# Row one-hots laid out by tile, a scan for the second half's places, and three first layers issued in a row

## The chip, the cores and the metric

The kernel runs on one core of one Trainium2 chip. The metric is device time in microseconds, the median of several executions. In the profile PE is TensorE (matmuls), PEld its weight loads, DVE is VectorE, ACT is ScalarE, POOL is GpSimd and SP is SyncE; a queue name such as POOLq is the engine's instruction sequencer.

## The reference

Attention without a softmax, and then a mixture of experts with one expert per token:

```
phi(x)  = outer product of S1 x and S2 x            # 8 x 8 = 64 features per head
kv, z   = sum over s of phi(k) v ,  sum of phi(k)   # 4 batches, 4 heads, 1088 positions, head_dim 32
x       = phi(q) kv / (phi(q) z + 1e-6)             # 4352 tokens x 128
expert  = argmax of cosine(x, expert_emb) / tau     # 8 experts
gate    = softmax of these logits at that expert
out     = gate * relu(x w1[expert]) w2[expert]      # 128 -> 1024 -> 128, float32
```

## The kernel before

**Two halves.** The four batches are worked as two halves (m = 0 and 1), each of 17 token tiles of 128 tokens. For each half the attention gives x and logits per token (steps `nd`, `x`), and a router finds each token's expert and its place in a list that is sorted by expert.

**The router** (`router`, line 728) works for half 0 on all 17 tiles at once and for half 1 on 8 and then on 9 tiles (`SPANS`). `best` and `pick` make a one-hot `oh` of the expert per token and its count `total`. `place` lets PE sum one-hots: `before` (a triangle of ones) times `oh` counts the tokens ahead in the same tile, and `ones` times shifted slices of `oh` adds the tiles ahead, one matmul per tile. `take` and `split` pick each token's own column out of the sum and split it into a block number `place_k` and a row `place_r`. `mark` compares `place_r` with the lane numbers and so writes `row`, a one-hot over 128 rows for every tile. In `row[P, P, tiles]` the tile number is the innermost index, 36 of them, so the 128 numbers of one tile lie 36 elements apart.

**The table** (`table`, lines 840 to 875). `sums` multiplies `row` of a tile (as weights, bfloat16, 128 x 128) with a few columns that carry the token numbers; summed over tiles that lists the tokens of each block. It is run once over 17 tiles for the first 10 blocks and once over 34 tiles for the other 25.

**The blocks.** 35 blocks of 128 tokens follow. Per block: `fetch` (POOL gathers the rows by an indirect DMA), `turn` (PE transposes them, DVE or ACT copies them out), `up` (first layer on PE, ReLU on ACT), `norm`, `shares`, `share` (the gate, on ACT, POOL and DVE) and `down` (second layer on PE, scaling on ACT, and an indirect DMA by POOL that scatters the result). Blocks 30, 31 and 32 are shared by two experts each (`two`, line 1069): `up` then uses column tiles of 64 with two weight sets, `down` column tiles of 32 (blocks 30 and 31) or 64 (block 32). Their second weights for `down` are copied by ACT (`second_weights_b`), into two buffers in turn.

**Order.** Nothing is scheduled by a planner: each step is put at a tick and a rank (`put_at`), ticks are emitted in order and ranks inside a tick, and every engine runs its instructions in the order in which they were emitted. Block i has tick 10 + i. In a tick the ranks are: `up` 30, `turn` of the next block 45, `shares` 60, `share` 73, `down` of the block before 74, `norm` of a later block 74.6, loads of weights 79. `fetch(34)` has rank 29 of block 30's tick. So on PE the order of the last blocks is up 30, turn 31, down 29, up 31, turn 32, down 30, up 32, turn 33, down 31, up 33, turn 34, down 32, up 34, down 33, down 34. Line 1256 puts a `drain` on POOL in block 32's tick, ahead of all other steps of that tick; on POOL the order is there: scatter 29, norm 33, scatter 30, norm 34, drain, scatter 31, 32, 33 and 34.

**The early part.** `ORDER` lists the steps of tick 4 by name. On DVE, ahead of half 1's feature product `qp 1`, come half 0's `take`, `split`, `rest`, the two `mark` and `find`; PE needs `qp 1` for the transposes `trqp 1`. `constants` (line 293) is the first step of all and `lanes` (line 330) stands after half 0's `total`.

Of the kernel before, what the change touches and what calls it, by code (L numbers as in the profile page):

```python
# [19 lines left out]
P = 128  # L20
# [51 lines left out]
def kernel(  # L72
# [195 lines left out]
    lane = consts.tile([P, P], F32, name="lane")  # L268
    lanes = consts.tile([P, P, WIDE], BF16, name="lanes")
    digits = consts.tile([P, 2, NM * NCP], BF16, name="digits")  # L270
# [10 lines left out]
    ones_e = consts.tile([P, E], F32, name="ones_e")  # L281
    oh = {(m, c): consts.tile([P, c1 - c, E], BF16, name=f"oh{m}_{c}") for m in range(NM) for c, c1 in SPANS[m]}
    total = {(m, c): consts.tile([P, E], BF16, name=f"total{m}_{c}") for m in range(NM) for c, _ in SPANS[m]}
# [46 lines left out]
    def wide_lanes():  # L330
        nc.vector.tensor_scalar_mul(lanes, bview(lane, [[1, P], [0, WIDE]]), 1.0 / P)

# [395 lines left out]
    def router(m, c0, c1, g, bank):  # L728
# [8 lines left out]
        def pick():  # L737

            t = work.tile([P, n, E], F32, tag=f"lt_{n}", name="lt")
# [4 lines left out]
            last["oh"] = nc.vector.tensor_tensor(out=oh[m, c0], in0=t, in1=mx.unsqueeze(2).broadcast_to([P, n, E]),  # L744
                                                 op=ALU.is_equal)
            with nc.allow_low_precision(reason="a count of at most SPAN is whole in bfloat16"):
                nc.vector.reduce_sum(out=total[m, c0], in_=oh[m, c0].rearrange("p j e -> p e j"), axis=AX.X)

        def place():

            hot = oh[m, c0]
            ps = s["ps"] = bank()[:, :n * E].rearrange("p (j e) -> p j e", e=E)
            mm(ps, before, hot, start=True, stop=False)
            for t in [base, less] + counts:
                mm(ps, ones, t.unsqueeze(1).broadcast_to([P, n, E]), start=False, stop=False)
            for j in range(1, n):
                mm(ps[:, j:], ones, hot[:, j - 1:j].broadcast_to([P, n - j, E]), start=False, stop=j == n - 1)
            counts.append(total[m, c0])  # L760

        def take():
            s["t"] = work.tile([P, n, E], F32, tag=f"lt_{n}", name="lt")
            nc.vector.tensor_mul(s["t"], s["ps"], oh[m, c0])

        def split():

            t0, t1 = m * NCP + c0, m * NCP + c1
            f = work.tile([P, n], F32, tag=f"mx8_{n}", name="mx8")
            nc.vector.reduce_sum(out=f, in_=s["t"], axis=AX.X)  # L770
            nc.vector.tensor_scalar(place_k[:, t0:t1], f, WHOLE, -WHOLE, op0=ALU.add, op1=ALU.add)
            nc.vector.scalar_tensor_tensor(out=place_r[:, t0:t1], in0=f, scalar=(P - 1) / (2.0 * P), in1=place_k[:, t0:t1],
                                           op0=ALU.add, op1=ALU.subtract)
# [54 lines left out]
    def table(which, m1, key):  # L828
# [21 lines left out]
        def sums():  # L850
            s["ps"] = ps_small()[:, :2 * n]
            tiles = [m * NCP + c for m in range(m1) for c in range(NC)]
            mm(s["ps"], ones, nowhere[which].rearrange("p d n -> p (d n)"), start=True, stop=False)
            for t in tiles:
                mm(s["ps"], row[:, :, t], s["col"].rearrange("p d n w -> p w d n")[:, t].rearrange("p d n -> p (d n)"),
                                 start=False, stop=t == tiles[-1])
# [46 lines left out]
    def plan_late():  # L903
# [94 lines left out]
        def extra():  # L998
# [29 lines left out]
            for t in tiles:  # L1028
                mm(ps, row[:, :, t], hit[:, 1:, t], start=False, stop=t == tiles[-1])
            with nc.allow_low_precision(reason="whole numbers of at most NOWHERE"):  # L1030
# [16 lines left out]
    def turn(i):  # L1047
        ps = ps_small()
        tp(ps[:, :P], xs[i][:, :DM], ident)
        xT[i] = work.tile([P, P], F32, tag="xTb", name="xTb")  # L1050
        (nc.scalar.copy if i < 2 or 4 <= i <= 8 else nc.vector.tensor_copy)(xT[i], ps[:, :P])  # L1051
# [17 lines left out]
    def two(i):  # L1069
        return FULL <= i < FULL + SHARED  # L1070
# [11 lines left out]
    def second_b(i):  # L1082
        return v_flat[1][:, i % 2 * F:(i % 2 + 1) * F]

# [7 lines left out]
    def up(i):  # L1092
        ps = ps_big()
        hT[i] = work.tile([P, 2, 512], F32, tag="kp", bufs=3, name="hT")
        x, w = xT.pop(i), wb.pop(i)
# [209 lines left out]
```

## Time and profile before

| | |
|---|---|
| runs | 196.45, 196.55, 197.93 us; median 196.55 us |
| profiled execution | 199.14 us, its span 197.2 us |
| PE busy | 188.3 us (95%), 2667 matmuls |
| PE weight loads | 177.8 us (90%) |
| POOL, ACT, DVE busy | 107.6, 99.1, 87.9 us |
| granted TensorE clock | 1.0 in every stretch read |

The span is what the trace shows of one execution; the profiled execution's own time is 1.94 us more, which lies around the span. Durations in the rows below are those of this one execution, whose time is above the median of the three others.

### The profile page before, as it was taken

How to read it: one execution, taken by the hardware profiler on the slowest of the kernel's cores; microseconds unless marked ns; L12 is line 12 of the kernel's file. 1: busy time of each engine (PE TensorE's matmuls, PEld its weight loads, DVE VectorE, ACT ScalarE, POOL GpSimd, SP SyncE). 2: the span in 40 equal slices, each digit the busy share in tenths (PEclk: the TensorE clock that was granted, in tenths of full speed). 3: DMA queues.
4: the chain of work that ended last, by engine and by line, in shares of the span. 5: the costliest groups of instructions: out<-in, count | busy, mean ns of one | idle time of the engine just before them, and what ended most of it. 6: DMA issues, size and time to landing. Idle time of an engine off the chain costs nothing.

```text
span 197.2 us, 7104 instructions
## 1 busy us (share of the span) xinstructions
PE 188.3 (95%) x2667; PEld 177.8 (90%) x2667; DVE 87.9 (45%) x393; ACT 99.1 (50%) x280; POOL 107.6 (55%) x135
## 2 busy tenths in 40 slices
PE   7999899999979999999999999999999999999990
PEld 7677799788869999999999999999999999998890
DVE  6589868798378489922221221221221221222100
ACT  2675542437253456433564654654654654766430
POOL 4300054707713866565977767767767767733052
PEclk9999999999999999999999999999999999999999
DMA  5979968974799997544587686596665655540001
GB/s 139 345 203 276 237 172 221 331 232 124 201 281 330 285 338 209 188 136 149 149 263 237 158 288 201 155 281 211 161 195 182 160 200 180 150 137 12 3 20 32
DMA packets 29924, 38.32 MB, mean 194 GB/s; under 512 B 5721, under 2 KB 23394, under 8 KB 29890
## 3 DMA queue, kind: packets, MB, share of 16 engines
q1 hardware_dynamic: 27600, 33.18, 56.3%
q0 software_dynamic: 2240, 4.67, 7.6%
q8 instruction: 23, 0.38, 0.8%
q14 instruction: 11, 0.09, 0.2%
q10 hardware_dynamic: 50, 0.01, 0.0%
HBM read 33.25 MB, written 4.66 MB: 192 GB/s over the span
## 4 chain that ended last, share of the span: by engine, by line
PE 75%; DMA 12%; DVE 6%; issue 2%; ACT 2%; POOLq 1%; POOL 0%
PE ps_big L155 35%; PE ps_acc L155 14%; PE ps_ab L155 14%; DMA xs<-rows,dst_i 12%; PE ps_t L158 6%; PE ps_t L155 3%; PE ps_acc L111 1%; DVE xg L679 1%; DVE row L779 1%; PE ps_ab L158 1%; PE ps_acc L158 1%; POOLq L1300 1%; DVE qp L458 1%; PE ps_big L158 1%; ACT hT L1108 1%
## 5 line engine op out<-in xcount | busy, mean ns | idle before, releaser
L155 PE MATMUL ps_big<-xTb,wb 128*128 128x128 f32 (+2 forms) x608 | 70.6, 266 | 0.1
L155 PEld LDWEIGHTS ps_big<-xTb,wb 128*128 128x128 f32 (+1 forms) x608 | 66.7, 183 | 1.5 <-issue 0.9
L1149 POOL DMA_INDIRECT out_dram<-y,dst_i x35 | 36.4, 1041 | 42.3 <-ACT sq L1113 21.4
L1108 ACT ACTIVATE hT<-ps_big 128x1024 f32<-128x1024 f32 x35 | 35.8, 1023 | 41.3 <-issue 23.6
L1043 POOL DMA_INDIRECT xs<-rows,dst_i x35 | 36.7, 1048 | 13.0 <-issue 6.1
L155 PE MATMUL ps_acc<-w_sb,hT 128*128 (+2 forms) x288 | 35.1, 275 | 0.0
L1051 DVE COPY xTb<-ps_t 128x128 f32<-128x128 f32 x28 | 8.1, 291 | 57.3 <-issue 39.7
L155 PEld LDWEIGHTS ps_acc<-w_sb,hT 128*128 128x128 f32 (+2 forms) x288 | 33.3, 184 | 0.3 <-issue 0.2
L155 PE MATMUL ps_ab<-w_sb,hT 128*128 (+1 forms) x272 | 33.2, 275 | 0.0
L155 PEld LDWEIGHTS ps_ab<-w_sb,hT 128*128 128x128 f32 (+1 forms) x272 | 31.6, 187 | 0.1
L1114 POOL TENSOR_TENSOR norm<-norm,half_c 128x1 f32<-128x1 f32 x35 | 20.7, 595 | 5.2 <-ACT sq L1113 4.9
L1127 DVE TENSOR_SCALAR gate<-gate 128x1 f32<-128x1 f32 x35 | 5.3, 150 | 21.2 <-ACT probs L1124 19.7
L458 POOL TENSOR_TENSOR kp<-both 128x1024 f32<-128x1024 f32 (+1 forms) x4 | 7.2, 1812 | 12.5 <-ACT both L499 11.1
L155 PE MATMUL ps_big<-kz,held 128*64 128x82 f32 x256 | 10.7, 236 | 1.1 <-ACT xTb L1051 1.1
L1146 ACT ACTIVATE y<-ps_ab,gate 128x128 f32<-128x128 f32 x17 | 6.2, 367 | 10.9 <-PE ps_ab L155 7.1
L155 PEld LDWEIGHTS ps_big<-kz,held 128*64 128x64 f32 x256 | 9.5, 136 | 2.3 <-ACT hT L1108 1.3
L1113 ACT ACTIVATE sq<-xs 128x128 f32<-128x128 f32 x35 | 10.6, 302 | 1.5 <-DMA xs<-rows,dst_i 1.3
L1124 ACT ACTIVATE probs<-xs,norm 128x8 f32<-128x8 f32 x35 | 10.3, 295 | 1.3 <-DVE norm L1118 1.3
L1146 ACT ACTIVATE y<-ps_acc,gate 128x128 f32<-128x128 f32 x17 | 6.2, 366 | 9.4 <-PE ps_acc L155 7.0
L158 PE MATMUL ps_t<-ident,xs 128*128 128x128 f32 x35 | 9.8, 279 | 0.0
L425 ACT COPY qT<-ps_t 128x512 f32<-128x512 f32 (+1 forms) x10 | 5.1, 535 | 7.2 <-PE ps_t L158 7.2
L458 DVE TENSOR_TENSOR kp<-both 128x1024 f32<-128x1024 f32 (+1 forms) x6 | 6.4, 1088 | 2.9 <-ACT both L499 2.8
(254 smaller groups left out, 254.4 us busy)
## 6 DMA issues: line engine op xcount, KB each, us to landing
wb<-in_moe_w_dram SPq DMA_DIRECT2D x35, 512.0 KB
w_sb<-in_moe_w_dram SPq DMA_DIRECT2D x16, 256.0 KB
rows<-xg SPq DMA_DIRECT2D x4, 544.0 KB
q<-in_q_dram SPq DMA_DIRECT2D x6, 256.0 KB
k<-in_k_dram SPq DMA_DIRECT2D x3, 512.0 KB
held<-in_moe_w_dram SPq DMA_DIRECT2D x3, 512.0 KB
v<-in_v_dram SPq DMA_DIRECT2D x2, 512.0 KB
v<-in_v_dram SPq DMA_DIRECT2D x4, 256.0 KB
```

The source lines that it names most:

```text
L155: last["pe"] = nc.tensor.matmul(*args, **how)
L158: last["pe"] = nc.tensor.transpose(*args)
L458: last[tag] = engine.tensor_mul(t.rearrange("p j h (i k) -> p (j h) i k", i=R), ab[:, :, 0].unsqueeze(3).broadcast_to([P, n * H, R, R]), b ...
L1043: nc.gpsimd.indirect_dma_start(out=xs[i][:], out_offset=None, in_=rows[:2 * S if t == 0 else N + 1], in_offset=bass.IndirectOffsetOnAxis(a ...
L1051: (nc.scalar.copy if i < 2 or 4 <= i <= 8 else nc.vector.tensor_copy)(xT[i], ps[:, :P])
L1108: nc.scalar.activation(hT[i], ps, ACT.Relu)
L1113: nc.scalar.activation(sq, xs[i][:, :DM], ACT.Square, accum_out=norms[i])
L1114: nc.gpsimd.tensor_tensor(out=norms[i], in0=norms[i], in1=half_c, op=ALU.pow)
L1124: nc.scalar.activation(p, xs[i][:, DM:], ACT.Exp, scale=norms.pop(i)[:, 0:1], accum_out=gate[i])
L1127: nc.vector.tensor_scalar_add(gate[i], gate[i], PROB_EPS)
L1146: nc.scalar.activation(y, ps, ACT.Copy, scale=gate.pop(i)[:, 0:1])
L1149: d = nc.gpsimd.indirect_dma_start(out=out[:, :], out_offset=bass.IndirectOffsetOnAxis(ap=dst_i[t][:, j:j + 1], axis=0), in_=y[:], in_offs ...
```

## The change

- `row` becomes `[P, tiles, P]`: the 128 numbers of a tile lie side by side. `place_r` holds each value twice and `lanes` shrinks from 128 x 10 to 128, so that `mark` can compare in pairs.
- For half 1, `oh` is laid out by expert and then tile. A scan along the tiles (`tensor_tensor_scan`, which restarts at each expert by a factor of 0 in `again`) gives running counts, `runs`; its last column is `total`. `place` then needs PE for the sum over tokens ahead in other lanes and over earlier spans alone, 8 columns wide: 4 matmuls for the first span and 5 for the second, in place of 11 and 13. DVE multiplies `runs` with `oh`, and `split` sums twice as many elements.
- The first layers of the shared blocks stand in a row. PE's order becomes up 29, turn 30, turn 31, down 28, turn 32, up 30, up 31, up 32, turn 33, turn 34, down 29, down 30, down 31, down 32, up 33, up 34, down 33, down 34. Block 32's transposed rows, its hidden layer and its second weights get places of their own; ACT's copies of second weights and one load of first weights come a tick earlier; the register loads for the shared blocks' second layers come before the down ahead of them.

```diff
-    lanes = consts.tile([P, P, WIDE], BF16, name="lanes")
+    lanes = consts.tile([P, P], BF16, name="lanes")
-    oh = {(m, c): consts.tile([P, c1 - c, E], BF16, ...)
+    oh = {(m, c): consts.tile([P, E, c1 - c] if m else [P, c1 - c, E], BF16, ...)
+    runs = {c: consts.tile([P, E, c1 - c], BF16, name=f"runs{c}") for c, c1 in SPANS[1]}
+    total = {(1, c): t[:, :, t.shape[2] - 1] for c, t in runs.items()}
-    place_r = consts.tile([P, NM * NCP], BF16, name="place_r")
-    row = consts.tile([P, P, NM * NCP], BF16, name="row")
+    place_r = consts.tile([P, NM * NCP, 2], BF16, name="place_r")
+    row = consts.tile([P, NM * NCP, P], BF16, name="row")
...
+        nc.vector.memset(upto_own, -(P + 1) / (2.0 * P))
+        for t in again.values():
+            nc.vector.memset(t, 1.0)
+            nc.vector.memset(t[:, :, :1], 0.0)
-        for t in (place_k, place_r):
-            nc.vector.memset(t, -1.0)
+        nc.vector.memset(place_k, -1.0)
...
 def pick():
+                if m == 0:
                     nc.vector.reduce_sum(out=total[m, c0], in_=oh[m, c0].rearrange("p j e -> p e j"), axis=AX.X)
+                else:
+                    nc.vector.tensor_tensor_scan(out=flat(runs[c0]), data0=flat(again[c0]), data1=flat(oh[m, c0]),
+                                                 initial=0.0, op0=ALU.mult, op1=ALU.add)
+        def place_by_runs():
+            ps = s["ps"] = bank()[:, :E]
+            mm(ps, before, total[m, c0], start=True, stop=False)
+            sums = [base, upto_own] + counts
+            for i, t in enumerate(sums):
+                mm(ps, ones, t, start=False, stop=i == len(sums) - 1)
+            counts.append(total[m, c0])
+            s["t"] = work.tile([P, 2, E, n], F32, tag=f"lt_{n}", bufs=1, name="pt")
+            nc.vector.scalar_tensor_tensor(out=s["t"][:, 0], in0=runs[c0], scalar=1.0 / P, in1=oh[m, c0],
+                                           op0=ALU.mult, op1=ALU.mult)
 def take():
+            if m == 1:
+                nc.vector.tensor_mul(s["t"][:, 1], oh[m, c0], s["ps"].unsqueeze(2).broadcast_to([P, E, n]))
+                s["t"] = s["t"].rearrange("p t e j -> p j (t e)")
+                return
 def mark(a=c0, b=c1):
-            w = b - a + (b - a) % 2
-            t0, t1 = m * NCP + a, m * NCP + a + w
-            nc.vector.tensor_tensor(out=row[:, :, t0:t1], in0=lanes[:, :, :w],
-                                    in1=bview(place_r[:, t0:t1], [[0, P], [1, w]]), op=ALU.is_equal)
+            w, t0 = b - a, m * NCP + a
+            nc.vector.tensor_tensor(out=row[:, t0:t0 + w].rearrange("p t (l d) -> p t l d", d=2),
+                                    in0=bview(lanes, [[0, w], [2, HALF], [1, 2]]),
+                                    in1=bview(place_r[:, t0:t0 + w], [[2, w], [0, HALF], [1, 2]]), op=ALU.is_equal)
 def sums():
-                mm(s["ps"], row[:, :, t], ...)
+                mm(s["ps"], row[:, t], ...)
 def turn(i):
+        if i == FULL + SHARED - 1:
+            xT[i] = v_rest[0][0][:, :H].rearrange("p h d -> p (h d)")
 def second_b(i):
-        return v_flat[1][:, i % 2 * F:(i % 2 + 1) * F]
+        m, u = ((1, 0), (1, 1), (0, 0))[i - FULL]
+        return v_flat[m][:, u * F:(u + 1) * F]
 def up(i):
+        if i == FULL + SHARED - 1:
+            hT[i] = v_flat[0][:, F:2 * F].rearrange("p (u n) -> p u n", u=2)
 def in_ticks(b0, b1, tick):
-                put(0, 29.9, lambda i=i: second_layers(i))
-                put(0, 30, lambda i=i: up(i))
-            if i + 1 < b1:
-                put(0, 45, lambda i=i: turn(i + 1))
+                to = put_at(tick + min(i, FULL) - b0) if two(i) else put
+                if two(i):
+                    put_at(tick + i - 1 - b0)(0, 73.8, lambda i=i: second_layers(i))
+                else:
+                    to(0, 29.9, lambda i=i: second_layers(i))
+                to(0, 30, lambda i=i: up(i))
+            j = i + 1
+            if 0 < j < b1:
+                to, rank = put, 45
+                if j == FULL + 1:
+                    to = put_at(tick + FULL - 1 - b0)
+                elif j == FULL + SHARED - 1:
+                    to, rank = put_at(tick + FULL - 1 - b0), 74.5
+                elif j >= FULL + SHARED:
+                    to, rank = put_at(tick + FULL - b0), 73.9
+                to(0, rank, lambda j=j: turn(j))
-                put(0, 74, lambda i=i: down(i - 1))
+                to = put_at(tick + min(i, FULL + SHARED - 1) - b0) if two(i - 1) else put
+                to(0, 74, lambda i=i: down(i - 1))
-                put(0, 79, lambda i=i: weights(i + 2))
+                to = put_at(tick + FULL - 1 - b0) if i + 2 == FULL + SHARED - 1 else put
+                to(0, 79, lambda i=i: weights(i + 2))
-                    put(1, 79, lambda i=i: second_weights_b(i + 2))
+                    put(0, 79, lambda i=i: second_weights_b(i + 2))
```

## Rows read from the trace of the kernel before

**Rows 1.** PE's waits: line, releaser, us in total, times, longest us.
```profile
PE ps_big L155 <- ACT xTb L1051: 1.1, 1, 1.1
```
**Rows 2.** Timeline of PE, half 1's second place: start us, us, instruction, count.
```profile
68.46 0.20 PE L155 MATMUL ps_big<-oh,before 128*128 128x72 bf16 x1
...
68.83 0.17 PE L155 MATMUL ps_big<-near,ones 128*128 128x8 bf16 x1
```
**Rows 3.** Timeline of PE, the second table's sums and the first layer behind them.
```profile
85.72 2.22 PE L155 MATMUL ps_t<-hits,row 128*128 128x56 bf16 x34
87.78 2.03 PE L155 MATMUL ps_big<-xTb,wb 128*128 128x128 f32 x16
```
**Rows 4.** Tile view of row: durations in ns, least, median, most; starts; forms.
```profile
L155 PEld LDWEIGHTS <-row x51: 137/169/180, 43.6 to 87.7; 128*128 128x128 bf16 x51
...
L779 DVE TENSOR_TENSOR row<-lanes,place_r x4: 684/762/818, 41.3 to 81.6; 128x1024 bf16<-128x1024 bf16 x2, 128x1280 bf16<-128x1280 bf16 x2
```
**Rows 5.** Timeline of PE's weight loads in half 1's first place.
```profile
64.45 0.34 PEld L155 LDWEIGHTS <-ones 128*128 128x128 bf16 x10
```
**Rows 6.** Timeline of DVE: start us, us, instruction [idle before, released by].
```profile
2.39 0.17 DVE L227 TENSOR_SCALAR s_w<-swords 16x32 uint32<-16x32 uint32 x1 [0.25 <-DMA swords<-in_S_dram]
...
26.31 1.23 DVE L458 TENSOR_TENSOR kp<-both 128x1024 f32<-128x1024 f32 x1 [1.47 <-ACT both L499]
...
41.28 1.42 DVE L779 TENSOR_TENSOR row<-lanes,place_r 128x1024 bf16<-128x1024 bf16 x2
...
82.82 1.19 DVE L848 TENSOR_TENSOR hits<-hits,digits 128x1008 bf16<-128x1008 bf16 x1
```
**Rows 7.** Timeline of PE where it waits for DVE's qp.
```profile
45.09 1.09 PE L158 MATMUL ps_big<-ident,qp 128*128 128x128 f32 x8 [0.27 <-DVE qp L458]
```
**Rows 8.** Timeline of PE over the last blocks.
```profile
169.28 0.24 PE L155 MATMUL ps_big<-xTb,wb 128*64 128x32 f32 x1
...
169.50 0.19 PE L155 MATMUL ps_big<-xTb,wb 128*64 128x32 f32 x1
...
171.19 0.19 PE L155 MATMUL ps_big<-xTb,wb 128*64 128x32 f32 x1
...
171.79 0.33 PE L158 MATMUL ps_t<-ident,xs 128*128 128x128 f32 x1
...
176.31 0.33 PE L158 MATMUL ps_t<-ident,xs 128*128 128x128 f32 x1
176.56 0.30 PE L155 MATMUL ps_acc<-w_sb,hT 128*32 x1
...
178.45 0.27 PE L155 MATMUL ps_big<-xTb,wb 128*64 128x64 f32 x1
...
180.70 0.33 PE L158 MATMUL ps_t<-ident,xs 128*128 128x128 f32 x1
...
188.72 1.95 PE L155 MATMUL ps_ab<-w_sb,hT 128*128 x16
190.51 1.95 PE L155 MATMUL ps_acc<-w_sb,hT 128*128 x16
```
**Rows 9.** POOL's drain by its line: durations in ns, least, median, most; start.
```profile
L1256 POOLq DRAIN  x1: 7095/7095/7095, 179.3 to 179.3; - x1
```
**Rows 10.** Timeline of POOL, the scatters of blocks 30 to 32 and 34.
```profile
179.25 1.04 POOL L1149 DMA_INDIRECT out_dram<-y,dst_i  x1 [3.04 <-ACT sq L1113]
...
187.26 1.01 POOL L1149 DMA_INDIRECT out_dram<-y,dst_i  x1 [6.36 <-issue]
188.58 0.98 POOL L1149 DMA_INDIRECT out_dram<-y,dst_i  x1 [0.30 <-issue]
...
193.15 0.97 POOL L1149 DMA_INDIRECT out_dram<-y,dst_i  x1 [0.82 <-DVE y L1144]
```
**Rows 11.** Timeline of ACT, scaling of block 29 and a copy of second weights.
```profile
173.94 0.37 ACT L1146 ACTIVATE y<-ps_ab,gate 128x128 f32<-128x128 f32 x1 [0.70 <-PE ps_ab L155]
...
174.50 1.03 ACT L1087 COPY v<-w_sb 128x1024 f32 x1
```

More of the change, by code (lines that the diff above doesn't have):

```diff
@@ L281 @@
     ones_e = consts.tile([P, E], F32, name="ones_e")
-    oh = {(m, c): consts.tile([P, c1 - c, E], BF16, name=f"oh{m}_{c}") for m in range(NM) for c, c1 in SPANS[m]}
-    total = {(m, c): consts.tile([P, E], BF16, name=f"total{m}_{c}") for m in range(NM) for c, _ in SPANS[m]}
+    oh = {(m, c): consts.tile([P, E, c1 - c] if m else [P, c1 - c, E], BF16, name=f"oh{m}_{c}")
+          for m in range(NM) for c, c1 in SPANS[m]}
+    runs = {c: consts.tile([P, E, c1 - c], BF16, name=f"runs{c}") for c, c1 in SPANS[1]}
+    total = {(1, c): t[:, :, t.shape[2] - 1] for c, t in runs.items()}
+    total[0, 0] = consts.tile([P, E], BF16, name="total0")
+    again = {c: consts.tile([P, E, c1 - c], BF16, name=f"again{c}") for c, c1 in SPANS[1]}
+    upto_own = consts.tile([P, E], BF16, name="upto_own")
     c_early = consts.tile([P, E + 1], F32, name="c_early")
@@ L330, in wide_lanes @@
     def wide_lanes():
-        nc.vector.tensor_scalar_mul(lanes, bview(lane, [[1, P], [0, WIDE]]), 1.0 / P)
+        nc.vector.tensor_scalar_mul(lanes, lane, 1.0 / P)
     def digits_of():
@@ L737, in pick @@
         def pick():
-            t = work.tile([P, n, E], F32, tag=f"lt_{n}", name="lt")
+            t = work.tile([P, 1 + m, n, E], F32, tag=f"lt_{n}", name="lt", **({"bufs": 1} if m else {}))[:, 0]
             mx = work.tile([P, n], F32, tag=f"mx8_{n}", name="mx8")
@@ L743, in pick, with flat @@
             nc.vector.reduce_max(out=mx, in_=t, axis=AX.X)
[L744 to L747, printed above, removed]
+            last["oh"] = nc.vector.tensor_tensor(out=oh[m, c0].rearrange("p e j -> p j e") if m else oh[m, c0], in0=t,
+                                                 in1=mx.unsqueeze(2).broadcast_to([P, n, E]), op=ALU.is_equal)
+            with nc.allow_low_precision(reason="a count of at most NC is whole in bfloat16"):
+                if m == 0:
+                    nc.vector.reduce_sum(out=total[m, c0], in_=oh[m, c0].rearrange("p j e -> p e j"), axis=AX.X)
+                else:
+                    nc.vector.tensor_tensor_scan(out=flat(runs[c0]), data0=flat(again[c0]), data1=flat(oh[m, c0]),
+                                                 initial=0.0, op0=ALU.mult, op1=ALU.add)
+        def flat(t):
+            return t.rearrange("p e j -> p (e j)")
+        def place_by_runs():
[8 more added lines that the diff above has]
+                                           op0=ALU.mult, op1=ALU.mult)
         def place():
+            if m == 1:
+                return place_by_runs()
             hot = oh[m, c0]
@@ L762, in take @@
         def take():
-            s["t"] = work.tile([P, n, E], F32, tag=f"lt_{n}", name="lt")
+            if m == 1:
+                nc.vector.tensor_mul(s["t"][:, 1], oh[m, c0], s["ps"].unsqueeze(2).broadcast_to([P, E, n]))
+                s["t"] = s["t"].rearrange("p t e j -> p j (t e)")
+                return
+            s["t"] = work.tile([P, 1, n, E], F32, tag=f"lt_{n}", name="lt")[:, 0]
             nc.vector.tensor_mul(s["t"], s["ps"], oh[m, c0])
@@ L771, in split @@
             nc.vector.tensor_scalar(place_k[:, t0:t1], f, WHOLE, -WHOLE, op0=ALU.add, op1=ALU.add)
-            nc.vector.scalar_tensor_tensor(out=place_r[:, t0:t1], in0=f, scalar=(P - 1) / (2.0 * P), in1=place_k[:, t0:t1],
+            nc.vector.scalar_tensor_tensor(out=place_r[:, t0:t1], in0=f.unsqueeze(2).broadcast_to([P, n, 2]),
+                                           scalar=(P - 1) / (2.0 * P),
+                                           in1=place_k[:, t0:t1].unsqueeze(2).broadcast_to([P, n, 2]),
                                            op0=ALU.add, op1=ALU.subtract)
         def mark(a=c0, b=c1):
-            w = b - a + (b - a) % 2
-            t0, t1 = m * NCP + a, m * NCP + a + w
-            nc.vector.tensor_tensor(out=row[:, :, t0:t1], in0=lanes[:, :, :w],
-                                    in1=bview(place_r[:, t0:t1], [[0, P], [1, w]]), op=ALU.is_equal)
+            w, t0 = b - a, m * NCP + a
+            nc.vector.tensor_tensor(out=row[:, t0:t0 + w].rearrange("p t (l d) -> p t l d", d=2),
+                                    in0=bview(lanes, [[0, w], [2, HALF], [1, 2]]),
+                                    in1=bview(place_r[:, t0:t0 + w], [[2, w], [0, HALF], [1, 2]]), op=ALU.is_equal)
         def write():
@@ L854, in sums @@
             for t in tiles:
-                mm(s["ps"], row[:, :, t], s["col"].rearrange("p d n w -> p w d n")[:, t].rearrange("p d n -> p (d n)"),
+                mm(s["ps"], row[:, t], s["col"].rearrange("p d n w -> p w d n")[:, t].rearrange("p d n -> p (d n)"),
                                  start=False, stop=t == tiles[-1])
@@ L1028, in extra @@
             for t in tiles:
-                mm(ps, row[:, :, t], hit[:, 1:, t], start=False, stop=t == tiles[-1])
+                mm(ps, row[:, t], hit[:, 1:, t], start=False, stop=t == tiles[-1])
             with nc.allow_low_precision(reason="whole numbers of at most NOWHERE"):
@@ L1049, in turn @@
         tp(ps[:, :P], xs[i][:, :DM], ident)
-        xT[i] = work.tile([P, P], F32, tag="xTb", name="xTb")
+        if i == FULL + SHARED - 1:
+            xT[i] = v_rest[0][0][:, :H].rearrange("p h d -> p (h d)")
+        else:
+            xT[i] = work.tile([P, P], F32, tag="xTb", name="xTb")
         (nc.scalar.copy if i < 2 or 4 <= i <= 8 else nc.vector.tensor_copy)(xT[i], ps[:, :P])
@@ L1093, in up @@
         ps = ps_big()
-        hT[i] = work.tile([P, 2, 512], F32, tag="kp", bufs=3, name="hT")
+        if i == FULL + SHARED - 1:
+            hT[i] = v_flat[0][:, F:2 * F].rearrange("p (u n) -> p u n", u=2)
+        else:
+            hT[i] = work.tile([P, 2, 512], F32, tag="kp", bufs=3, name="hT")
         x, w = xT.pop(i), wb.pop(i)
@@ L1221, in in_ticks @@
             if i < b1:
-                put(0, 29.9, lambda i=i: second_layers(i))
-                put(0, 30, lambda i=i: up(i))
-            if i + 1 < b1:
-                put(0, 45, lambda i=i: turn(i + 1))
+                to = put_at(tick + min(i, FULL) - b0) if two(i) else put
+                if two(i):
+                    put_at(tick + i - 1 - b0)(0, 73.8, lambda i=i: second_layers(i))
+                else:
+                    to(0, 29.9, lambda i=i: second_layers(i))
[10 more added lines that the diff above has]
+                to(0, rank, lambda j=j: turn(j))
             if i < b1:
```

## The prediction

> **What bounds the kernel now.** I read the busy shares first: PE is busy 95% of the span, the others about half. Then PE's waits: its longest one behind the warm-up of the first microseconds is 1.1 us [rows 1], and the timeline shows no other of size. So from about 45 us on, PE's own work is the path, and what is taken from PE there comes off the end, as long as nothing else takes over. Two places break that rule. Between 38 and 45 us DVE is the path: it runs without a gap through half 0's take, split, marks and table, and PE waits 0.27 us for `qp 1` behind them [rows 7]. And at the very end the path is PE, then the scaling, then POOL's scatter of block 34 at 193.15 [rows 10], 0.85 us behind PE's last matmul (190.51 plus 1.79, the distance of the last two second layers [rows 8], is 192.30). From that scatter to the end of the span lie 4.05 us that no edit touches. The drain on POOL, 7.1 us long [rows 9], is off the path now: scatter 31 begins 8.01 us after scatter 30, two scatters in a row are 1.32 us apart [rows 10], so the queue alone would allow scatter 34 at 179.25 + 8.01 + 3 x 1.32 = 191.2. It has 1.9 us to spare.
>
> **The change part by part.**
>
> *The sums over 34 tiles.* 34 matmuls with `row` as weights take 87.78 - 85.72 = 2.06 us, 61 ns each [rows 3]. Their columns can't explain that: the 13 matmuls of half 1's second place, up to 72 columns wide, stand 0.37/13 = 28.5 ns apart [rows 2]. What differs is the weight load: 169 ns for `row` [rows 4], while ten loads of `ones`, whose numbers lie side by side, take 0.34 us together, as the union of overlapping loads [rows 5]. If the new layout brings `row` to the pace of `ones`, 34 x (61 - 28.5) = 1.09 us go, on PE's path. The bounds are 0 (the loads stay as they are) and 1.09; I take 1.09, since the other layout is the one visible difference. The first 17 sums shorten too, but PE only waits longer for `qp 1` there: nothing.
>
> The Trainium skill, "TensorE: Matmul & The Clock Gate", section "Weight-path perf modes", speaks against this: it lets the fast weight load apply to every non-FP32 load of 128 columns whose column step is between -1,023 and 1,024 elements, packed or strided. By that rule the old loads, at a step of 36, are fast already and nothing is won. The 169 ns row does not look like it, so I keep that as a rival.
>
> *Places.* 7 + 8 = 15 matmuls fewer at 28.5 ns: 0.43 us off PE's path. On DVE a scan replaces a sum over at most 72 elements, one product per span is added, and `split` sums twice as much: some 0.2 us each, for two spans. DVE waits for PE in this stretch, and after it the last product for the table ends at 84.01 [rows 6], 1.7 us before PE needs it at 85.72 [rows 3]; with PE 0.43 earlier 1.3 us of cover remain. Nothing; without that cover about 0.6 us.
>
> *Marks.* The trace has no compare in pairs. The old rows give (818 - 684)/256 = 0.52 ns per element above a fixed part [rows 4]. The new marks have 1024 and 1152 elements (the padding column goes). At the old pace half 0's pair loses 0.06 us, which I don't count; at twice that time per element it grows from 1.52 to 2.60, 1.08 us longer, all on DVE's path ahead of `qp 1`. I take no change, as both forms hold 16-bit neighbours.
>
> *Constants and lanes.* Five more small memsets and one less stand at the start, where DVE waits 0.25 us for the sketches' DMA; the smaller `lanes` frees DVE before 26.31, where it waits 1.47 us for ACT anyway [rows 6]. Both nothing; without the first cover a few tenths.
>
> *The moved transposes.* Turns 31 and 32 now precede up 30. One matmul of that size takes 1.79/16 = 0.11 us [rows 8]: 0.22 us later. Up 30 now starts at T = 169.28 [rows 8]; afterwards at T' = 169.28 - 1.09 - 0.43 + 0.22, 1.30 us earlier.
>
> *The row of three.* Six starts of a repeated group in up 30 span 171.19 - 169.50 = 1.69 us, 0.282 us each, so its eight would take 2.25; it took 2.51 up to the transpose [rows 8]. The 0.26 us at its end I read as the array running empty before it changes its tile shape. Ups 30 and 31 no longer pay it; up 32 does (2.25 us as now). A transpose followed by another shape costs 0.25, so 0.14 for the change [rows 8]. The new PE order then runs, from T': ups 2.25 + 2.25 + 2.25; turns 33 and 34 0.36; down 29 1.79, change 0.14; downs 30, 31 and 32 1.75 + 1.75 + 1.89 (block 30's now lasts 1.89 with the change behind it); two ups and two downs 7.16. Sum 21.59, against 192.30 - 169.28 = 23.02 now. The bounds of the two tails are 0 and 0.26 each. ACT's ReLU (about 1 us) fits beside the next up, with two buffers; SP's earlier load waits on blocks long done.
>
> *What is late next.* PE would let scatter 34 start at T' + 21.59 + 0.85 = T' + 22.4. But POOL's order is kept: scatter 30, norm 34, drain, scatters 31 to 34. Down 30 now ends only at T' + 10.8 instead of about T + 9.2. ACT scales block 29 at about T' + 9.1, does a square and a copy of weights, which end 1.59 us after the scaling's start [rows 11], then the gate of block 31 and the scaling of block 30, together some 0.8 us: T' + 11.5, scatter 30 at T' + 11.8. With today's distances scatter 34 comes at T' + 11.8 + 8.01 + 3 x 1.32 = T' + 23.8, against T + 23.87 now. POOL takes over by 1.3 us, and the row of three wins nothing at the end.
>
> **The sum.** 1.30 at T' and 0.1 behind it: 1.4 us. Against the profiled execution of 199.14 that is 197.7; its time is 2.6 above the median of the runs, so I take the difference to the median: 196.55 - 1.4 = **195.15 us**.
>
> **Rivals.**
>
> *POOL does not bind.* If the drain is not a fixed cost but ends with something else, or is shorter when it begins later, PE sets the end: 1.30 + 23.87 - 22.4 = 2.75 us, 193.8 us. For it: the scatter ahead of the drain and a norm are over long before the drain ends, so what it waits for is not seen [rows 9, 10]. Against it: no semaphore of another engine releases the instruction behind it, the wait is put down to issue. Chance 0.25.
>
> *The layout does nothing for weight loads.* Then T' is only 0.21 us earlier and the whole gain is 1.4 - 1.09 = 0.3: 196.25. It is the page's rule above as this kernel's mechanism; the 169 ns against `ones` speaks against it. Chance 0.10.
>
> *Marks at half the pace.* 1.08 us are given back on DVE's path: 0.3 us, 196.25. Half 1's marks, as much longer, just fit the 1.3 us of cover. Chance 0.06. The Trainium skill, "VectorE: DVE Perf Modes", section "What auto-detection actually checks", gives the double rate to 16-bit tensors with step 1 in each, which the pairs keep; no run here shows it.
>
> *Slower: marks at a quarter of the pace.* If every pair costs DVE a restart, say 2.1 ns per element, half 0's marks grow by 3.4 us ahead of `qp 1`, and half 1's by as much, of which 1.3 are covered: -1.4 + 3.4 + 2.1 = +4.1, 200.6 us. It decides from about 0.7 us more per mark on, in half 0. Nothing shows such a price. Chance 0.06.
>
> **How the numbers follow.** The forecast has 0.50; 0.03 are left for what I don't see. Its own range is 194.6 (ACT sooner, the drain a little shorter) to 195.9 (both tails stay, another 0.5). The range 193.7 to 196.5 takes in the forecast, POOL not binding, and the two cases that leave 0.3 us. About 1% (1.97 us) is what a measurement of this kernel can tell from no change: faster holds POOL not binding and the fringe of the forecast, 0.28; slower the last rival, 0.06; within 1% the rest, 0.66.
>
> **What would show it.** The 34 sums in about 1 us, loads of `row` near 100 ns; up 30, 31 and 32 with 2.25 us from start to start; the drain again 7 us, ending after block 31's scaling by several us, and scatters 31 to 34 evenly 1.3 us apart with the last one more than a microsecond behind the last scaling. If instead scatter 34 follows that scaling by 0.3 us, the step on POOL is wrong, and the time is nearer 193.8. If PE waits long before `trqp 1`, the marks are.

## The result and the profile after

In the comparison that the prediction was made for, the changed kernel took 195.57 us (median of 8 runs, 194.64 to 199.58) against 197.06 for the kernel before (8 runs). The ratio is 0.988, with a 95% interval of 0.985 to 0.992: the changed kernel is 2.3 us faster, 1.7 to 3.0. (The ratio is that of the fast runs, while the two medians and some of the profiled executions hold slow ones; from up 2 on, where the stretches below begin, the granted clock is 1.0 in every profile up to about scatter 34.) Three later groups of runs, each on one chip beside the kernel before, gave the changed kernel 1.001 (0.996 to 1.006), 0.988 (0.981 to 0.994) and 1.002 (0.998 to 1.006). So the gain appears in two comparisons and is absent in two, and that needs explaining too.

The profiled execution of the changed kernel has a span of 197.5 us. How long the first stages take differs between executions of one and the same kernel: PE starts up 2 of the kernel before at 62.65 us in its first profile and at 66.40 in a later one. I therefore compare stretches that begin at up 2, which starts at 65.18 us here.

First the tile view of `row` (durations in ns: least, median, most; starts; forms) in the changed kernel:

```profile
L155 PEld LDWEIGHTS <-row x51: 95/96/98, 46.7 to 88.7; 128*128 128x128 bf16 x51
...
L809 DVE TENSOR_TENSOR row<-lanes,place_r x4: 672/717/751, 43.3 to 83.9; 128x1024 bf16<-128x1024 bf16 x2, 128x1152 bf16<-128x1152 bf16 x2
```

A load of `row` takes 96 ns instead of 169, and the marks keep their pace: 751 ns for 1152 elements, where 1280 took 818 [rows 4].

The timeline of PE (start us, busy us, instruction, count) has the 34 sums and half 1's second place:

```profile
70.86 0.18 PE L155 MATMUL ps_big<-runs,before 128*128 128x8 bf16 x1
...
71.00 0.17 PE L155 MATMUL ps_big<-near,ones 128*128 128x8 bf16 x1
...
87.89 1.04 PE L155 MATMUL ps_t<-hits,row 128*128 128x56 bf16 x34
88.84 2.02 PE L155 MATMUL ps_big<-xTb,wb 128*128 128x128 f32 x16
...
170.55 0.24 PE L155 MATMUL ps_big<-xTb,wb 128*64 128x32 f32 x1
```

The sums take 88.84 - 87.89 = 0.95 us, against 2.06 [rows 3]; the place takes 0.14 us, against 0.37 [rows 2]. From up 2 to up 30, which starts at 170.55, are 105.37 us, against 169.28 - 62.65 = 106.63 [rows 8].

The timeline of POOL at the end (in brackets its idle time before, and what ended it) answers to [rows 10], and the view of the drain's line to [rows 9]:

```profile
179.98 1.02 POOL L1187 DMA_INDIRECT out_dram<-y,dst_i  x1 [5.97 <-ACT y L1184]
181.01 0.60 POOL L1152 TENSOR_TENSOR norm<-norm,half_c 128x1 f32<-128x1 f32 x1
181.92 1.04 POOL L1187 DMA_INDIRECT out_dram<-y,dst_i  x1 [0.31 <-ACT sq L1151]
182.98 0.59 POOL L1152 TENSOR_TENSOR norm<-norm,half_c 128x1 f32<-128x1 f32 x1
189.93 1.01 POOL L1187 DMA_INDIRECT out_dram<-y,dst_i  x1 [6.36 <-ACT probs L1162]
191.25 0.98 POOL L1187 DMA_INDIRECT out_dram<-y,dst_i  x1 [0.30 <-ACTq L1312]
192.54 0.98 POOL L1187 DMA_INDIRECT out_dram<-y,dst_i  x1 [0.30 <-issue]
193.82 0.98 POOL L1187 DMA_INDIRECT out_dram<-y,dst_i  x1 [0.30 <-DVEq L1312]
```
```profile
L1308 POOLq DRAIN  x1: 7100/7100/7100, 182.0 to 182.0; - x1
```

Scatter 31 again begins 8.01 us behind scatter 30, and the last three follow 1.3 us apart with 0.30 us of idle time each, the pace of a queue that has work waiting (this row of scatters behind the drain is called the ladder below). PE and DVE were done well before, as their timelines show:

```profile
190.22 1.95 PE L155 MATMUL ps_acc<-w_sb,hT 128*128 x16
```
```profile
192.47 0.35 DVE L1182 TENSOR_SCALAR y<-ps_acc,gate 128x128 f32<-128x128 f32 x1 [2.15 <-PEq L1312]
```

The last block is scaled by 192.82, and its scatter starts at 193.82. So POOL now ends last: 1.0 us lie between the two, where the handover by itself takes 0.35 (e1 below). From scatter 34 to the end of the span are 3.68 us, against 4.05.

### The profile page after: what moved, and what is told of

The parts are those of the page before. It is cut to its first block, busy times and chain, and to the rows that moved or that the text cites. A ratio compares the mean times of both kernels' runs of the same rounds, so it can differ in the third digit from the quotient of the medians.

```text
span 197.5 us, 7080 instructions
## 1 busy us (share of the span) xinstructions
PE 185.8 (94%) x2652; PEld 176.1 (89%) x2652; DVE 88.9 (45%) x399; ACT 98.9 (50%) x280; POOL 105.8 (54%) x135
## 4 chain that ended last, share of the span: by engine, by line
PE 71%; DMA 15%; issue 4%; DVE 4%; POOL 2%; ACT 2%; POOLq 1%; SPq 0%; DVEq 0%; ACTq 0%
PE ps_big L155 30%; PE ps_acc L155 16%; PE ps_ab L155 14%; DMA xs<-rows,dst_i 12%; PE ps_t L158 6%; DMA w_sb<-in_moe_w_dram 4%; PE ps_t L155 2%; PE ps_acc L111 1%; DVE xg L687 1%; POOLq L1352 1%; PE ps_ab L158 1%; PE ps_acc L158 1%; DVE qp L466 1%; POOL norm L1152 1%; POOL out_dram L1187 1%
## 5 line engine op out<-in xcount | busy, mean ns | idle before, releaser
L155 PE MATMUL ps_big<-xTb,wb 128*128 128x128 f32 (+1 forms) x576 | 67.4, 268 | 0.8 <-DMA wb<-in_moe_w_dram 0.7
L155 PEld LDWEIGHTS ps_big<-xTb,wb 128*128 128x128 f32 (+1 forms) x576 | 64.2, 186 | 1.5 <-PE ps_big L155 0.9
L1187 POOL DMA_INDIRECT out_dram<-y,dst_i x35 | 35.5, 1015 | 43.3 <-ACT y L1184 21.1
L1146 ACT ACTIVATE hT<-ps_big 128x1024 f32<-128x1024 f32 x34 | 34.8, 1024 | 39.8 <-PE ps_big L155 39.8
L1074 POOL DMA_INDIRECT xs<-rows,dst_i x35 | 35.6, 1016 | 12.5 <-issue 6.1
L155 PE MATMUL ps_acc<-w_sb,hT 128*128 (+1 forms) x272 | 33.2, 275 | 0.4 <-DMA w_sb<-in_moe_w_dram 0.4
L155 PEld LDWEIGHTS ps_acc<-w_sb,hT 128*128 128x128 f32 (+1 forms) x272 | 31.6, 187 | 0.7 <-DMA w_sb<-in_moe_w_dram 0.6
L155 PE MATMUL ps_big<-kz,held 128*64 128x82 f32 x256 | 11.6, 248 | 0.0
L155 PEld LDWEIGHTS ps_big<-kz,held 128*64 128x64 f32 x256 | 10.4, 146 | 1.3 <-issue 1.2
L158 PE MATMUL ps_t<-ident,xs 128*128 128x128 f32 x35 | 9.3, 276 | 0.0
```

The lines of the kernel that those rows point to most:

```text
L155: last["pe"] = nc.tensor.matmul(*args, **how)
L158: last["pe"] = nc.tensor.transpose(*args)
L1074: nc.gpsimd.indirect_dma_start(out=xs[i][:], out_offset=None, in_=rows[:2 * S if t == 0 else N + 1], in_offset=bass.IndirectOffsetOnAxis(a ...
L1146: nc.scalar.activation(hT[i], ps, ACT.Relu)
L1187: d = nc.gpsimd.indirect_dma_start(out=out[:, :], out_offset=bass.IndirectOffsetOnAxis(ap=dst_i[t][:, j:j + 1], axis=0), in_=y[:], in_offs ...
```

## The experiments

Every profiled kernel is cut into the same three stretches: up 2 to up 30, up 30 to scatter 34, scatter 34 to the end of the span. Starts come from the timelines, and the last stretch from the span. The ratio is that of timed runs to the kernel before, with its 95% interval.

```
kernel                 up2-up30  up30-s34  s34-end    sum    ratio
before, first page       106.63     23.87     4.05  134.55
changed, first page      105.37     23.27     3.68  132.32   0.988 (0.985-0.992)
group 1  a1_changed      106.67     24.35     4.14  135.16   1.001 (0.996-1.006)
         e1_drain_early  106.00     23.31     4.05  133.36   1.003 (0.998-1.008)
         e2_no_drain     107.31     24.89     7.62  139.82   1.026 (1.019-1.032)
         e3_two_drains   107.13     23.93     4.26  135.32   not timed
group 2  b2_before       106.69     23.44     4.07  134.20
         a2_changed      105.37     23.26     3.73  132.36   0.988 (0.981-0.994)
         e4_layout_alone 105.57     23.44     4.10  133.11   0.994 (0.990-0.998)
         e5_row_alone    106.91     23.26     3.70  133.87   0.998 (0.994-1.001)
group 3  b3_before       106.69     23.86     4.20  134.75
         a3_changed      105.98     24.35     4.28  134.61   1.002 (0.998-1.006)
         e6_no_row       105.77     23.86     3.99  133.62   0.999 (0.995-1.003)
         e7_drain_early  107.46     23.31     4.01  134.78   1.000 (0.996-1.005)
```

### Group 1: is POOL's drain what binds?

Beside the changed kernel (a1) stand three with its drain moved, taken out and doubled.

> The changed kernel as it is, to compare the others with. If POOL sets the end: scatter 34 again about 1.0 us behind the scaling of block 34 (0.3 us in the kernel before), scatters 31 to 34 1.3 us apart, the drain 7.1 us. If PE sets the end: scatter 34 0.3 us behind that scaling. Against the kernel before about -2 us by the stretch from block 2's first layer to the end of the span (134.6 us before, 132.3 us after); -1.4 us by the forecast.

> The changed kernel with POOL's drain moved from block 32's tick to block 30's, right behind the last gather, where POOL is idle for 6 us. If the drain is what makes the last scatter late: scatter 34 0.3 us behind the scaling of block 34, so 0.7 us less than the changed kernel (195.4 -> 194.7), and the drain still 5 to 6 us long behind the gather's end. If PE alone sets the end, or if the drain ends with something late in the program rather than with what is ahead of it: no change, within 0.2 us, or a drain that lasts until about 186 to 189.

```diff
-    put_at(first + USUAL - AHEAD + 1)(0, 29.5, lambda: nc.gpsimd.drain(fusable=False))
+    put_at(first + FULL)(0, 29.5, lambda: nc.gpsimd.drain(fusable=False))
```

> The changed kernel without that drain. If a drain's length grows with the gathers and scatters since the last one (5.5 us behind POOL's last work with 66 of them, 1.5 to 1.8 us with 4 at the end of the program: 0.06 us each and 1.4 us), the drain at the end of the program takes about 5.7 us behind scatter 34 in place of 1.5, and the kernel is 3.4 us slower than the changed one. If it is a fixed price of that one instruction, the end is 0.7 us earlier than in the changed kernel and nothing is paid later.

```diff
-    put_at(first + USUAL - AHEAD + 1)(0, 29.5, lambda: nc.gpsimd.drain(fusable=False))
```

> The changed kernel with two drains, in the ticks of blocks 20 and 30. If the length grows with the gathers and scatters since the last drain: the first (44 of them) ends about 4.1 us behind POOL's last work, the second (20) about 2.6 us. If it is fixed: both 5 to 5.5 us. The time matters little here.

```diff
-    put_at(first + USUAL - AHEAD + 1)(0, 29.5, lambda: nc.gpsimd.drain(fusable=False))
+    for block in (20, FULL):
+        put_at(first + block)(0, 29.5, lambda: nc.gpsimd.drain(fusable=False))
```

With the drain ahead of scatter 30 the ladder is gone. POOL's and DVE's timelines of e1:

```profile
185.41 1.01 POOL L1187 DMA_INDIRECT out_dram<-y,dst_i  x1 [0.57 <-ACT y L1184]
187.38 0.98 POOL L1187 DMA_INDIRECT out_dram<-y,dst_i  x1 [0.96 <-ACT y L1184]
192.51 0.98 POOL L1187 DMA_INDIRECT out_dram<-y,dst_i  x1 [4.15 <-ACTq L1312]
194.35 0.98 POOL L1187 DMA_INDIRECT out_dram<-y,dst_i  x1 [0.86 <-DVE y L1182]
```
```profile
193.65 0.35 DVE L1182 TENSOR_SCALAR y<-ps_acc,gate 128x128 f32<-128x128 f32 x1 [1.89 <-PE ps_acc L155]
```

POOL waits 4.15 us ahead of scatter 33, and scatter 34 follows the scaling by 0.35 us. It comes 23.31 us behind up 30 instead of 24.35 in a1. That does not show that the drain sets the end in a1, because scatter 34 does not follow scatter 33 at the queue's pace there. POOL's timeline of a1:

```profile
193.71 0.98 POOL L1187 DMA_INDIRECT out_dram<-y,dst_i  x1 [0.30 <-issue]
195.36 0.97 POOL L1187 DMA_INDIRECT out_dram<-y,dst_i  x1 [0.67 <-issue]
```

Scatter 34 starts 0.28 us behind the last scaling, which ends at 195.08 (its line is in group 3), and a3 has the same 0.28: by the sign named beforehand, POOL does not set the end in these two. At the queue's pace of 1.28 us it could have started at 194.99, 23.98 us behind up 30. So 0.67 of the 1.04 us is the ladder's, and the other 0.37 is a scaling that came late (group 3). POOL does set the end on the first page of the changed kernel, in a2 and in e5, with scatter 34 1.0 us behind the scaling; no execution of that kind had its drain moved.

e2 shows what the drain saves: without it the closing drain, 3.1 us in a1, takes 7.0, and the kernel ends 7.62 us behind scatter 34, 3.5 us more than in a1 for 3.4 foreseen; it is 2.6% slower than the kernel before. Scatter 34 itself came no sooner than in a1: it starts 1.62 us behind its scaling, for a reason that the trace does not name. The views of the drains' lines (durations in ns: least, median, most), of e2 and of e3:

```profile
L1351 POOLq DRAIN  x3: 40/113/6995, 195.3 to 202.8; - x3
```
```profile
L1309 POOLq DRAIN  x2: 4715/5818/6921, 134.4 to 171.9; - x2
```

e3's first drain took 6921 ns, its second, ten ticks later, 4715. Part of each is POOL's own work, still running when the drain is issued; the last of it are these gathers:

```profile
135.60 1.01 POOL L1074 DMA_INDIRECT xs<-rows,dst_i  x1 [0.18 <-issue]
...
173.15 1.01 POOL L1074 DMA_INDIRECT xs<-rows,dst_i  x1 [0.18 <-issue]
```

Counted from their ends, the drains last 4.7 us, with 44 gathers and scatters since the last drain, and 2.5 us, with 20. Counted in the same way, the drain of the first pages lasts 5.5 us (66), e1's 5.6 (64), e2's closing drain 5.8 us (70), and the closing drains of the other kernels 1.5 to 2.1 us (4 or 6). So the length grows with what was sent, as the theory of growing lengths had it (4.1 and 2.6 us for e3). In e3, and in it alone, ups 26 to 28 stand 3.94 us apart instead of 3.68, so a drain among the full blocks is not free either.

Timed, e1 was no faster than a1 (1.003 and 1.001), nor was e7, the same kernel in group 3, faster than a3 (1.000 and 1.002), though in the profiles the end comes 1.1 and 1.3 us sooner behind up 30. Each of the two differences is uncertain by about 0.6%, as much as the profiles promise; together they speak against the whole of that gain and don't settle how much of it there is. No version is shown to beat the changed kernel.

### Group 2: the parts by themselves

> The kernel before, once more, for a profile of it beside the other runs of this group. Two theories of why the changed kernel gained 2.3 us in the first comparison and nothing in the second. Gift taken back: where gathers and TensorE's own issue are late, the 0.5 us saved at the second half's places turn into a wait for the gathered rows ahead of ups 4 and 9, so here those two waits are absent or shorter by 0.3 to 0.5 us than in the changed kernel (which had 0.4 to 1.0 and 0.5), and up 2 to up 30 takes 106.6 us plus at most 0.3. Equal disturbance: the same waits stand here too, as long, and up 2 to up 30 takes 107.5 to 108.5 us.

> The changed kernel again, to see which of the two comparisons holds. Gain is real (-1.3 us ahead of up 30, -0.6 to -1.0 in the last row): a ratio of 0.988 to 0.994, with scatter 34 about 23.3 us behind the start of up 30. Gift taken back: a ratio of 0.997 to 1.003, with waits of 0.4 us or more ahead of ups 4 and 9 and gaps put down to issue inside the downs of blocks 30 to 32.

> The kernel before with the new layout of row, lanes and place_r alone. If strided weight loads were the cost, the 34 sums take 1.0 us instead of 2.06, up 30 starts 1.1 us sooner (up 2 to up 30 in 105.5 us without disturbances), and as the last row is unchanged all of it shows: a ratio of 0.994. If a fast load already covered the old layout, 1.000 and sums of 2.06 us. If waits for gathers take it back, sums of 1.0 us and a ratio of 0.998 to 1.002.

e4 is the kernel before with the layout alone, which takes the new `lanes`, `place_r` and `mark` along:

```diff
-    row = consts.tile([P, P, NM * NCP], BF16, name="row")
+    row = consts.tile([P, NM * NCP, P], BF16, name="row")
...
-                mm(s["ps"], row[:, :, t], s["col"].rearrange("p d n w -> p w d n")[:, t].rearrange("p d n -> p (d n)"),
+                mm(s["ps"], row[:, t], s["col"].rearrange("p d n w -> p w d n")[:, t].rearrange("p d n -> p (d n)"),
...
```

> The kernel before with the row of three first layers alone (old layout, old places). My prediction: up 30 starts 0.2 us later, POOL's ladder (scatter 30, drain, three scatters) brings scatter 34 at 23.3 to 23.8 us behind it against 23.9 now, so 0.2 us slower to 0.4 us faster: a ratio of 0.998 to 1.001. If the two vanished tails came through at the end: 1.2 us faster, 0.994. If gaps in the dense downs of blocks 30 to 32 are the price of the row: 0.5 to 1.0 us slower, 1.003 to 1.005.

e5 is the kernel before with `turn`, `second_b`, `up` and `in_ticks` of the changed one: old layout, old places.

```diff
-                put(0, 30, lambda i=i: up(i))
-            if i + 1 < b1:
-                put(0, 45, lambda i=i: turn(i + 1))
+                to = put_at(tick + min(i, FULL) - b0) if two(i) else put
...
+                to(0, 30, lambda i=i: up(i))
...
+                to(0, rank, lambda j=j: turn(j))
```

The tile view of `row` in e4 and in e5:

```profile
L155 PEld LDWEIGHTS <-row x51: 95/96/99, 46.0 to 87.6; 128*128 128x128 bf16 x51
```
```profile
L155 PEld LDWEIGHTS <-row x51: 138/163/173, 45.7 to 88.4; 128*128 128x128 bf16 x51
```

Here the parts add up. Against b2, the layout takes 1.12 us off the way to up 30 and nothing behind it, 1.09 in all, and 1.2 is timed (0.4 to 2.0). The row of three puts up 30 0.22 us later, brings scatter 34 0.18 us nearer and the end 0.37 nearer, 0.33 us faster in all, and 0.4 is timed, an interval that holds no change. The changed kernel sums to 1.84, and 2.5 is timed (1.2 to 3.7). What the two parts leave of the way to up 30 in a2 is the second half's places: 1.32 - 1.12 + 0.22 = 0.42 us. The starts of the first layers show the same directly: from up 2 to up 3 and from up 3 to up 4 b2 takes 4.08 and 4.29 us, a2 3.90 and 4.06, together 0.41 us less.

### Group 3: where the gain goes

> The kernel before once more, for a profile beside the others of this group. So far: up 2 to up 30 in 106.63 and 106.69 us, up 30 to scatter 34 in 23.87 and 23.44, scatter 34 to the end in 4.05. If this group runs undisturbed as the second did, the same again within 0.1 us up to up 30. If it is disturbed as the first was: waits for gathered rows ahead of ups 4 and 9 here too say that both kernels pay them; none here, but some in the changed kernel, say that the time saved at the second half's places turns into them.

> The changed kernel, a third time, as the measure for the next one. Additive theory (layout 1.1, places 0.4, row of three 0.4 at the end, less 0.2 for the moved transposes): ratio 0.988 to 0.990, up 2 to up 30 in 105.4 us, scatter 34 at 23.3 us behind up 30. Rival, a gain that waits take back: ratio 0.997 to 1.002.

> The changed kernel with POOL's drain moved ahead by some ticks, right behind the last gather. If POOL's ladder sets the end of the changed kernel by 0.93 us, as its rows say, scatter 34 follows the scaling of its block at 22.3 us behind up 30 against 23.3; the closing drain, which now waits behind scatter 34's own wait, gives back 0.35 us: 0.6 us faster than the changed kernel, a ratio to before of 0.985. If the drain is only paid elsewhere (a longer closing drain, scatters 29 to 31 late): no faster than the changed kernel, 0.988 or above.

> The changed kernel with the old last row: layout and the second half's places alone. Additive theory: 1.1 + 0.4 sooner at up 30, so up 2 to up 30 in 105.15 us (0.2 less than in the changed kernel, whose transposes stand ahead of up 30), then 23.4 and 4.05 us as before: 1.5 us faster, ratio 0.992. If the places' 0.4 us do not come through: 105.55 us and 0.994.

e7 has the diff of e1. e6 is the changed kernel with e5's edit undone, that is with the old `turn`, `second_b`, `up` and `in_ticks`:

```diff
-                to = put_at(tick + min(i, FULL) - b0) if two(i) else put
...
-                to(0, 30, lambda i=i: up(i))
...
+                put(0, 30, lambda i=i: up(i))
+            if i + 1 < b1:
+                put(0, 45, lambda i=i: turn(i + 1))
```

The program of a3 is that of a2, but 2.3 us more are spent from up 2 on. The first place is ahead of up 9. PE's and DVE's timelines of a2:

```profile
90.46 0.27 PE L158 MATMUL ps_t<-ident,xs 128*128 128x128 f32 x1
...
92.66 1.95 PE L155 MATMUL ps_big<-xTb,wb 128*128 128x128 f32 x16
```
```profile
90.77 0.29 DVE L1085 COPY xTb<-ps_t 128x128 f32<-128x128 f32 x1 [1.78 <-PE ps_t L158]
```

The same of a3:

```profile
89.41 0.27 PE L158 MATMUL ps_t<-ident,xs 128*128 128x128 f32 x1
...
92.12 2.05 PE L155 MATMUL ps_big<-xTb,wb 128*128 128x128 f32 x16 [0.34 <-DVE norm L1155]
```
```profile
91.78 0.29 DVE L1085 COPY xTb<-ps_t 128x128 f32<-128x128 f32 x1 [3.48 <-PE ps_ab L155]
```

In a2 DVE copies the transpose 0.04 us behind its end, in a3 2.10 us behind it, although DVE is idle and its next instruction is the same. ACT is as late: its ReLU of up 8 starts 2.17 us behind the end of that first layer (87.55 + 2.02), where a2 has 0.04.

```profile
91.74 1.02 ACT L1146 ACTIVATE hT<-ps_big 128x1024 f32<-128x1024 f32 x1 [4.60 <-PE ps_ab L155]
```

Up 9 starts when the copy is there, not when PE is free; from up 8 to up 10 a3 takes 0.6 us more than a2. All seven kernels of groups 1 and 3 that have the new layout show this wait; b3, with the old one, does not. By the sign named for b3, part of the time saved ahead of up 9 turns into a wait here: a3 reaches up 30 0.61 us later than a2.

The second place is the last row. PE's timeline of a1:

```profile
181.42 0.38 PE L155 MATMUL ps_acc<-w_sb,hT 128*32 x2
181.94 0.38 PE L155 MATMUL ps_acc<-v,hT 128*32 128x128 f32 x4
...
183.76 0.38 PE L155 MATMUL ps_ab<-v,hT 128*32 128x128 f32 x4
184.42 0.31 PE L155 MATMUL ps_acc<-w_sb,v 128*64 x1 [0.27 <-issue]
...
191.78 1.95 PE L155 MATMUL ps_acc<-w_sb,hT 128*128 x16
```

The last second layer starts 191.78 - 171.01 = 20.77 us behind up 30, against 190.22 - 170.55 = 19.67 on the first page of the changed kernel. Most of the difference lies in the small matmuls of blocks 30 to 32, inside which PE pauses at 181.5 and at 184 without a releaser that the trace names ("issue"). Then DVE's timeline of a1:

```profile
194.73 0.35 DVE L1182 TENSOR_SCALAR y<-ps_acc,gate 128x128 f32<-128x128 f32 x1 [2.85 <-PE ps_acc L155]
```

The last scaling starts 1.00 us behind PE's end (191.78 + 1.95 = 193.73), where it took 0.30 on the first page. Both last stretches of a1 and a3 are the same to 0.2 us.

This second lateness may be of another kind than the first. In a1 and a3 the scaling starts 0.04 to 0.05 us behind the end of POOL's scatter 33 (193.71 + 0.98 = 194.69 in a1). In all fourteen profiles it is late where a scatter of POOL's is running when PE ends (a1, a3, a2 and the first page of the changed kernel, 0.28 to 1.00 us), and starts 0.04 us behind PE where none is. What would link the two engines no run shows; it is no general rule, since a2's copy at 90.77 starts inside a gather of POOL's (89.80 to 90.81).

I call executions in which ACT or DVE sees PE's first layers this late ones with late handovers. The kernel before pays less in them. b3 reaches up 30 in the same 106.69 us as b2 and loses 0.42 us to scatter 34 and 0.13 at the end; its ReLU of block 10 starts 0.75 us behind the end of the first layer (98.50 against 95.80 + 1.95). The first page of the kernel before is such an execution too: ACT's timeline there shows block 10's ReLU 0.71 us behind the end of its first layer (95.53 + 1.95 by PE's timeline),

```profile
98.19 1.02 ACT L1108 ACTIVATE hT<-ps_big 128x1024 f32<-128x1024 f32 x1 [1.37 <-PE ps_t L158]
```

and in b2 the same ReLU starts 0.04 us behind it (99.34 + 1.95):

```profile
101.33 1.02 ACT L1108 ACTIVATE hT<-ps_big 128x1024 f32<-128x1024 f32 x1 [0.69 <-PE ps_big L155]
```

PE had other work there, so the kernel before lost nothing by it. The two outcomes add up from the stretches: without late handovers, b2 to a2, -1.84 us; with late handovers, b3 to a3, -0.71 to up 30, +0.49 to scatter 34 and +0.08 at the end, together -0.14, where 1.002 (-0.4 to +1.1 us) was timed.

What makes PE's completions late in some groups stays open. It is not the granted clock, which is 1.0 from up 2 up to the last slice in a2 and a3 alike, and not the chip, which is the same in groups 2 and 3. One mark separates the two kinds of executions: the profile pages of five executions (the first of the changed kernel, b2, a2, e4 and e5) give the loads of `wb` a median time to landing (3.6 to 4.1 us), and those of the other nine, all with late handovers, give none, as the recorder has fewer records of landings there (2616 in a2, 1592 in a3). The line in the pages of a2 and a3:

```profile
wb<-in_moe_w_dram SPq DMA_DIRECT2D x35, 512.0 KB, 4.1
```
```profile
wb<-in_moe_w_dram SPq DMA_DIRECT2D x35, 512.0 KB
```

Whether the recording disturbs these executions, or loses records because they are disturbed, no run tells; a pause put down to "issue" in them may have a releaser whose record is missing. I can't undo it in a kernel, and each kernel has one profile in a group. e6 fits only in part: its stretches are 1.13 us shorter than b3's, its timed ratio allows 1.0 at most. e7 waited another 0.9 us for `xTb` ahead of up 4, as did e2 (1.1), a1 and e3 (0.3 each), and not a3 or e1, so a single profile carries about a microsecond of chance there.

## Why the prediction was right, step by step

- *Sums over 34 tiles, -1.09.* Right: 2.06 to 0.95 us on the first page, and 1.12 us of the way to up 30 by e4 alone. The two bounds were 0 and 1.09, and it is the upper one. The rival by which the layout does nothing falls with it. That rival was a rule of the Trainium skill, "TensorE: Matmul & The Clock Gate", section "Weight-path perf modes", which lets the fast weight load apply at a column step of 36 too; this case disagrees, with 169 ns for a load at that step and 96 ns at a step of 1.
- *Places, -0.43.* Right: 0.42 by difference in group 2, and 0.41 by the starts of ups 2 to 4. The scan takes its place on DVE without a wait of PE's.
- *Marks, 0.* Right: 672 to 751 ns. Both rivals on slower marks fall, the one on the slower side included. The Trainium skill's "VectorE: DVE Perf Modes", "What auto-detection actually checks", gives the double rate where every tensor is 16-bit with a step of 1; these rows agree in so far as the pairs keep the pace of the old form, 672 ns for 1024 elements against 684.
- *Transposes moved ahead, +0.22.* Right: e5 shows 106.91 against 106.69. The way to up 30 came out at -1.26 on the first pages and -1.32 in group 2, for -1.30.
- *PE's row of three.* 21.59 us foreseen from up 30 to PE's end, 190.22 + 1.79 - 170.55 = 21.46 found. The two tails vanish: up 32 starts at 175.08, 4.53 us behind up 30, for twice 2.25 foreseen.
- *POOL takes over.* Right in kind: the drain is again 7.1 us, the ladder again 8.01 us, the last scatters are even, and scatter 34 starts 1.0 us behind the last scaling, on the first page as in a2 and e5. e1 and e7 remove the ladder by moving the drain, but beside a1 and a3, in which the late scaling ends last. Scatter 30 came 11.37 us behind up 30 for 11.8 foreseen: ACT's timeline has block 30's scaling at 181.25, 10.70 us behind up 30 for 11.5. The rival in which POOL does not bind falls for the executions without late handovers. In a1 and a3 scatter 34 does follow the scaling by 0.28 us, but not for that rival's reason: the drain lasts 7.1 us there as well.
- *The sum, -1.4.* This is the term that was too small. "0.1 behind it" is 0.52 us without late handovers (group 2: 0.18 to scatter 34, 0.34 behind it). Most of that is the stretch that I took as fixed, the 4.05 us "that no edit touches". On the first pages it is 3.68 against 4.05. The profiles show one difference there, the closing drain. Its line in the first page of the changed kernel and in b2:

```profile
L1352 POOLq DRAIN  x3: 46/113/3419, 192.9 to 197.2; - x3
```
```profile
L1300 POOLq DRAIN  x3: 46/113/3043, 196.3 to 200.3; - x3
```

Where scatters follow without a break it is issued 0.9 us ahead of scatter 34 (193.82), where POOL waits for the scaling 0.2 us ahead (196.53 in b2). It then ends 2.5 us behind that scatter's start instead of 2.8. No experiment changed that alone. That 195.57 lies so near to 195.15 is in part luck: the gain was 2.3 us for 1.4 foreseen, and the kernel before had a median of 197.06 beside it for the 196.55 that the forecast started from.

- *What it did not see.* The first page of the kernel before was taken with late handovers in it: scatter 34 stands 23.87 us behind up 30, where b2 has 23.44. In such executions the changed kernel gains nothing, and no rival had that.

## What to carry to other kernels

Lay out weights so that the numbers of one load lie side by side: here it bought 1.1 us for 34 loads, the largest part of the gain, and a tile view shows the price at once. When PE's last row is made denser, cost the queue behind it by its own ladder, since a drain that was free can become the end, as it did here where no handover was late. Compare a change by stretches that begin behind the noisy part, in more than one group of runs: one group alone would have told of 1.2% or of nothing.

## What was not expected of the hardware

- The length of POOL's drain grows with what was sent since the last one: behind POOL's last work it takes 5.5 to 5.8 us after 64 to 70 gathers and scatters, 4.7 after 44 and 2.5 after 20 (e3), and 1.5 to 2.1 after 4 to 6.
- The same program ran from up 2 to its end in 132.4 us in one group and 134.6 in another, with PE's completions seen by ACT and DVE up to 2.2 us late (up 8 in a3).
